# An adaLN block: chunk 2's statistics into a product buffer, chunk 5's norm and DMA transpose placed earlier, chunk 7's turns on TensorE

## The chip, the cores and the metric

The kernel runs on one core of one Trainium2 chip. The metric is the device time in microseconds (us) of one execution. The core has five engines that run their own queues of instructions in order: PE (TensorE, the matrix unit; its weight loads are listed apart as PEld), DVE (VectorE), ACT (ScalarE), POOL (GpSimd) and SP (SyncE, here a queue that issues DMAs). POOL issues DMAs too. SBUF is the working memory with 128 partitions; PSUM has eight banks, in which PE leaves its results.

## The reference

```
mod = silu(c) @ w_mod                      # six rows of 576: sa, ca, ga, sb, cb, gb
h = layernorm(x) * (1 + ca) + sa           # x: 2048 x 576
qkv = h @ wqkv                             # 32 heads of 18
attn = softmax over 8 keys at positions s, s-2, ..., s-14 of q.k / sqrt(18)
x = x + ga * ((attn . v) @ wo)
h = layernorm(x) * (1 + cb) + sb
x = x + gb * (((h @ w_gate) * (h @ w_up)) @ w_down)     # 576 -> 4608 -> 576
```

## The kernel before

**Tiling.** The 2048 rows are eight chunks of 256 rows (`CH`), each of two tiles of 128 (`ST`). The attention goes chunk by chunk; the second half (the GLU) goes by five groups of row tiles, `GROUPS` (line 45): 2, 4, 4, 3 and 3 tiles. For each group `gate_up` (line 879) runs 36 steps f over the 4608 columns, and then `down_pairs` (line 936; `down_last` for the last group) multiplies by `w_down`, in steps n: 32 or 48 steps and a last block of four f. Nearly all matmuls are pairs: one on rows 0 to 63 of the array and one on rows 64 to 127, side by side.

**The order of the work is written out by hand.** The program is compiled with a manual schedule: each engine keeps the order in which the code emits its instructions, and the waits between engines follow from the tiles. The attention of later chunks is woven into the GLU of earlier groups. `gbg[gi]` (lines 1397 to 1401) is a list of pieces with costs; `spread` (line 869) places them over the 36 steps of `gate_up` by running cost. `units` (lines 1508 to 1510) puts q, k and v projections of later chunks behind given steps f. `dbg[gi]` (lines 1496 to 1507) puts pieces behind given steps n of `down_pairs`. So a number such as 27 in `(27, a_flip(4))` is a place in the emitted order, not a time: an engine with nothing else in its queue may come to the piece earlier.

**Pieces.** `a_` pieces belong to the first layernorm and the projections of a chunk, `b_` pieces to the attention and the second layernorm, `o_` to the attention's output. A normalised chunk (tile `ln_xn`) has to be transposed before it can be multiplied. There are two ways. A *turn* is done on PE: `turn_unit` (line 606) makes 20 transposes of 64x64 output blocks for two row tiles, 12 in its first part and 8 in its second, into two PSUM banks (`tr_pA`, `tr_pB`), and its evictions by ACT and DVE also apply the modulation (`o_parts`, `a_parts`, `b_parts`). A *flip* is a DMA transpose on SP's queue, one for each row tile (`flips`, line 690, with `o_flip`, `a_flip`, `b_flip`), and the modulation comes later, in place (`a_mod`, `b_mod`). The attention's logits are transposed the same two ways: `b_lq` (line 480) leaves them in `lgs` and, for chunks over 2, issues a flip to `lgt`; for chunks 1 and 2 `b_lt` (line 501) makes eight transposes on PE and two ACT copies.

**Buffers.** `lnp` (line 78) has two buffers for `ln_xn`; chunks over 2 also put their eighth product there (line 467 on, `b_p`). `prodp` has six product buffers, `hTp` one `hT`, `h2p` one `h2T`, and `psp` the eight PSUM banks. When a tile is made, the compiler gives it a buffer that an earlier tile has given back, and the first instruction that writes the new tile waits for the last readers of the old one.

**Around the change.** Near the end of group 0's `down_pairs`, `norm_x1_2` (line 1479) computes chunk 2's second layernorm: row tile 0's mean and squares on ACT (`act_norm`, line 306, which uses its own output tile `xn` as the place for the values that nobody reads), row tile 1's on DVE, and then the norm of both on DVE. Two evictions of chunk 3's values follow on ACT (`v1_3`), then chunk 1's turns (`b_parts(1)`, places 27 and 28), the flips of chunk 4's norm (`a_flip(4)`, place 27) and chunk 2's own turns (`t2_2`, from place 30). In group 1's `gate_up`, `B_both` (line 853) goes through chunks 3 and 4: products, logits, softmax (`B_sm`), weighted values; chunk 5's first layernorm (`a_ln(5)`, `a_norm(5)`) comes behind chunk 3's weighted values and its flips in chunk 4's softmax, and its projections at f = 29 to 33. In group 3's `down_pairs` come chunk 7's output flips, its projection `w7` by `wo`, its layernorm and flips, and the flip of chunk 6's second row tile. With three row tiles this stage holds six PSUM banks (`acc` and `accr`) and has two left.

Of the kernel before, what the change touches and what calls it, by code (L numbers as in the profile page):

```python
# [18 lines left out]
P = 128  # L19
D = 576  # L20
# [21 lines left out]
MODK = (0, 4, 1, 2, 3)  # L42
QKK = (0, 1, 4, 2, 3)
PAIRED = (3, 4, 5, 6, 7)
GROUPS = [(0, 2), (2, 6), (6, 10), (10, 13), (13, 16)]


@with_exitstack
def kernel(
# [253 lines left out]
        nc.scalar.activation(rstd, rstd, ACTF.Ln, bias=eps[:], scale=1.0 / D)  # L303
        nc.scalar.activation(rstd, rstd, ACTF.Exp, scale=-0.5)

    def act_norm(src):
        xn = lnp.tile([P, ST, DP], BF, name="ln_xn")
        mv = small.tile([P, ST, 2], F32, name="ln_mva")

        def mean(j):  # L310
            nc.scalar.activation(xn[:, j, 0:D], src(j), ACTF.Identity, scale=-1.0 / D, accum_out=mv[:, j, 0:1])

        def square(j):
            nc.scalar.activation(xn[:, j, 0:D], src(j), ACTF.Square, bias=mv[:, j, 0:1], accum_out=mv[:, j, 1:2])

        def rsq(r=slice(0, ST)):
            nc.scalar.activation(mv[:, r, 1], mv[:, r, 1], ACTF.Ln, bias=eps[:], scale=1.0 / D)
            nc.scalar.activation(mv[:, r, 1], mv[:, r, 1], ACTF.Exp, scale=-0.5)

        def norm(j):  # L320
            for d0, s0, n in ((0, 0, D), (D, D - 64, 64)):
                nc.vector.tensor_scalar(xn[:, j, d0:d0 + n], src(j)[:, s0:s0 + n], mv[:, j, 0:1], mv[:, j, 1:2], ALU.add, ALU.mult)
        return xn, mean, square, rsq, norm
# [156 lines left out]
    def b_lq(i, wq):  # L480
        b = bb[i]
        if wq == 0:
            b["lg"] = ps([P, 2, CH], F32, "lg")
        for m in range(KT):
            for wl in range(4):
                nc.tensor.matmul(b["lg"][H * wl:H * (wl + 1), wq, :], lhsT=ind[:, m, :], rhs=b["prod"][4 * wq + wl][:, m, :],  # L486
                                 start=(m == 0), stop=(m == KT - 1), skip_group_check=True)
        for wl in range(4):
            b["prod"].pop(4 * wq + wl)
        if wq == 1:  # L490
            lgs = lgp.tile([P, 2, CH], BF, name="lgs")
            nc.scalar.copy(lgs[:], b.pop("lg")[:])
            b["lgt"] = lgp.tile([P, 2, ST, 4, H], BF, name="lgt")
            if i > 2:
                nc.sync.dma_start_transpose(out=b["lgt"][:].rearrange("p a j w h -> p (a j) (w h)"), in_=lgs[:].rearrange("p a t -> p (a t)"))
            else:
                b["lgs"] = lgs
# [1 line left out]
    LO, HI = slice(0, 64), slice(64, P)  # L499

    def b_lt(i):
        if i > 2:
            return
        b = bb[i]
        lgs = b.pop("lgs")
        pts = [ps([P, 2 * ST, 64], BF, "lt") for _ in range(2)]
        for a in range(2):
            for j in range(ST):
                for pt, r in zip(pts, (LO, HI)):
                    nc.tensor.transpose(pt[:, ST * a + j, :], lgs[r, a, js(j)], ident[r, r])  # L510
        for k, pt in enumerate(pts):
            nc.scalar.copy(b["lgt"][:].rearrange("p a j w h -> p (a j) (w h)")[:, :, 64 * k:64 * (k + 1)], pt[:])
# [191 lines left out]
    def a_mod(i):  # L704
        return lambda: in_place(aa[i]["hT"], 0, KT)
# [127 lines left out]
    def B_pr(i, w0, w1):  # L833
        return [(0.83, lambda w=w: b_p(i, w)) for w in range(w0, w1)]
# [14 lines left out]
    def b_lqs(i):  # L849
        b_lq(i, 0)  # L850
        b_lq(i, 1)

    def B_both(first, a, b, av_a, av_b, *turned):
        return (B_pr(a, 0, 3) + [(0.0, p) for p in first] + B_pr(a, 3, 8) + B_wait(1.5) + [(0.0, lambda: b_lqs(a))] + B_wait(1.5) + B_pr(b, 0, 8) + B_wait(1.5)
                + B_sm(a, lambda: b_lqs(b)) + av_a + B_sm(b, *turned) + av_b)

    def B_one(a, ld, av_a):
        return (B_pr(a, 0, 4) + ld[:1] + B_pr(a, 4, 8) + ld[1:] + B_wait(1.5) + [(0.0, lambda: b_lqs(a))] + B_wait(4.0) + B_sm(a) + av_a)
# [530 lines left out]
    def values(i):  # L1389
        return [(0.0, lambda: [b_ld(i, j) for j in range(ST)])]  # L1390

    av1 = B_av(1)
    for k, p in ((13, lambda: n3["square"](1)), (11, lambda: mean3(1)), (8, lambda: n3["square"](0)), (5, lambda: mean3(0))):
        av1.insert(k, (0.0, p))
    av4 = B_av(4)
    av4.insert(6, (0.5, a_mod(5)))
    gbg = {0: B_two(1, 2, av1 + [res(2), (0.0, load_wm5), (0.0, lambda: load_wd(0))], []),
           1: values(3) + B_both([a_mod(4)], 3, 4, B_av(3) + [res(3), res(4), (2.4, lambda: a_ln(5)), (1.2, lambda: (a_norm(5), load_x(7)))], av4, o_flip(3), a_flip(5)),
           2: values(5) + B_both((), 5, 6, B_av(5) + [res(5), res(6)], B_av(6), nop, o_flip(5)),
           3: B_one(7, [(0.0, lambda: b_ld(7, 0)), (0.0, lambda: behind(b_ld(7, 1), wgu_in[3 * NBLK + 4]))], B_av(7)) + [res(7)],  # L1400
           4: [(1.0, nop), (1.0, early_wd)]}
    av2 = [p for _, p in B_av(2)]
# [74 lines left out]
        n4["rsq"]()  # L1477

    def norm_x1_2():
        begin(n2, lambda j: x1[2][j][:])  # L1480
        xn = bb[2]["xn"] = n2["xn"]
        stats, mv = small.tile([P, ST, 2, 6], F32, name="ln_statsb"), small.tile([P, ST, 2], F32, name="ln_mvb")
        stat_act(n2, (0,))
        n2["rsq"](slice(0, 1))
        for hf in range(2):
            nc.vector.bn_stats(stats[:, 1, hf, :], x1[2][1][:, hf * 288:(hf + 1) * 288])
# [3 lines left out]
        n2["norm"](0)  # L1490
        for d0, s0, n in ((0, 0, D), (D, D - 64, 64)):
            nc.vector.tensor_scalar(xn[:, 1, d0:d0 + n], x1[2][1][:, s0:s0 + n], mv[:, 1, 0:1], mv[:, 0, 1:2], ALU.subtract, ALU.mult)
# [56 lines left out]
```

## Time and profile before

| | us |
|---|---|
| three runs | 552.82, 561.39, 565.06 |
| their median | 561.39 |
| the profiled execution | 557.14 |
| its span, first to last instruction | 555.4 |
| `gate_up`, group 0 (from 47.1) | 39.6 |
| `down_pairs`, group 0 (from 86.7) | 40.7 |
| `gate_up`, group 1 (from 127.4) | 89.4 |
| `down_pairs`, group 1 (from 216.8) | 39.7 |
| `gate_up`, group 2 (from 256.5) | 79.2 |
| `down_pairs`, group 2 (from 335.7) | 39.7 |
| `gate_up`, group 3 (from 375.4) | 61.0 |
| `down_pairs`, group 3 (from 436.4) | 35.7 |
| `gate_up`, group 4 (from 472.1) | 52.7 |
| `down_last` (from 524.8) | 30.6 |

How the lines are read: in a timeline a line gives the start in us, the length in us, the engine, the line of the code, the operation, output <- inputs, and how many equal instructions are merged (x4, say); the bracket at its end is the idle time of the engine ahead of it and what ended that. In a view by stretches of time each engine has its busy time and (x) its instructions, then the granted share of PE's clock (PEclk; 1.00 is full), the busy share of the DMA engines and what they moved. In the list of waits each line is an engine's instruction and what it waited for, with the total in us, the number of times and the longest.

### The profile page before, as it was taken

What the parts mean: (1) busy time and instruction counts of PE and PEld (TensorE: products, weight loads), DVE (VectorE), ACT (ScalarE), POOL (GpSimd) and SP (SyncE); (2) the same over time, 40 slices, a digit from 0 to 9 for tenths busy, and PEclk for the clock granted to TensorE, in tenths of its full rate; (3) what the DMA queues carried; (4) which work ended last, traced back from release to release, by engine and by line L of the source; (5) the groups of instructions that cost most, each with busy time, mean ns of one, the idle gap of its engine ahead of it and who ended that gap; (6) DMA issues with size and microseconds to landing.
All of it is one profiled execution on the core that took longest, in us unless ns stands there. A gap on an engine that the chain in (4) does not pass through costs nothing.

```text
span 555.4 us, 16882 instructions
## 1 busy us (share of the span) xinstructions
PE 533.4 (96%) x7253; PEld 341.7 (62%) x7259; DVE 317.5 (57%) x775; ACT 256.1 (46%) x617; POOL 71.1 (13%) x117
## 2 busy tenths in 40 slices
PE   7999999959999979999999999999999979999997
PEld 5788886635544456656644445557655768777664
DVE  7887899747369855656366795725429322422202
ACT  2766787644655654111655552205556301455500
POOL 4301223021000000122000101111100112200010
PEclk9999999979999999999999999999999989999999
DMA  8999998969265945966635896763896858965021
GB/s 275 271 294 313 355 295 285 336 130 334 80 172 180 292 119 170 181 173 215 225 109 139 269 261 151 181 165 106 271 245 218 206 134 229 318 212 182 2 87 33
DMA packets 92310, 114.05 MB, mean 205 GB/s; under 512 B 25770, under 2 KB 79994, under 8 KB 92234
## 3 DMA queue, kind: packets, MB, share of 16 engines
q1 hardware_dynamic: 80976, 67.00, 44.3%
q0 software_dynamic: 11168, 45.81, 26.6%
q8 instruction: 57, 0.93, 0.7%
q14 instruction: 19, 0.16, 0.1%
q10 hardware_dynamic: 90, 0.15, 0.1%
HBM read 103.22 MB, written 4.48 MB: 194 GB/s over the span
## 4 chain that ended last, share of the span: by engine, by line
PE 83%; DMA 6%; issue 4%; DVE 3%; ACT 2%; SPq 1%; POOL 1%; ACTq 0%; POOLq 0%
PE pg L563 26%; PE pu L563 21%; PE acc L563 15%; PE pp L563 8%; PE acc L1078 3%; PE accr L563 2%; DMA wgu<-in_B_w_up_dram 2%; PE lg L486 2%; DMA hT<-ln_xn 1%; DMA wqk<-in_A_wqkv_dram 1%; SPq L692 1%; DMA wd<-in_B_w_down_dram 1%; DVE prod L476 1%; PE pq L415 1%; PE po L791 1%
## 5 line engine op out<-in xcount | busy, mean ns | idle before, releaser
L563 PE MATMUL pg<-h2T,wgu 64*128 64x512 bf16 (+2 forms) x1440 | 280.3, 334 | 0.0
L563 PE MATMUL pu<-h2T,wgu 64*128 64x512 bf16 (+2 forms) x1440 | 276.2, 334 | 0.2 <-DMA wgu<-in_B_w_up_dram 0.2
L563 PEld LDWEIGHTS <-wgu 64*128 64x128 bf16 x2880 | 148.4, 94 | 99.1 <-issue 0.7
L906 ACT CAST u_sb<-pu 128x512 bf16<-128x512 f32 (+2 forms) x180 | 90.1, 501 | 141.2 <-PE pg L563 133.0
L912 DVE TENSOR_TENSOR hh<-g_sb,u_sb 128x512 bf16<-128x512 bf16 (+2 forms) x180 | 66.3, 370 | 106.5 <-ACT g_sb L907 104.6
L563 PE MATMUL acc<-wd,hh 64*128 64x512 bf16 x888 | 117.2, 380 | 0.7 <-DMA wd<-in_B_w_down_dram 0.6
L563 PEld LDWEIGHTS <-hh 64*128 64x128 bf16 x1872 | 75.7, 96 | 41.8 <-issue 2.0
L907 ACT CAST g_sb<-pg 128x512 bf16<-128x512 f32 (+2 forms) x180 | 91.5, 509 | 0.0
L563 PE MATMUL accr<-wd,hh 64*128 64x64 bf16 x888 | 85.5, 191 | 0.0
L563 PE MATMUL pu<-h2T,wgr 64*128 64x512 bf16 (+2 forms) x180 | 60.2, 335 | 0.0
L563 PE MATMUL pg<-h2T,wgr 64*128 64x512 bf16 (+2 forms) x180 | 60.2, 334 | 0.0
L173 POOL DMA_DIRECT2D wd<-in_B_w_down_dram x38 | 28.8, 758 | 172.1 <-PE accr L563 94.3
L476 DVE TENSOR_TENSOR prod<-qT,kT 128x1280 bf16<-128x1280 bf16 x54 | 42.9, 820 | 7.8 <-ACT kT L393 7.8
L548 DVE TENSOR_TENSOR vsh<-vsh,attn 128x1152 bf16<-128x1152 bf16 x56 | 40.2, 751 | 0.0
L563 PEld LDWEIGHTS <-wgr 64*128 64x128 bf16 x360 | 19.8, 94 | 13.8 <-issue 2.0
L661 DVE TENSOR_TENSOR x<-pp,ga_bc 128x288 bf16<-128x288 f32 x28 | 12.0, 452 | 25.0 <-PE pp L563 25.0
L563 PE MATMUL pp<-hT,wqk 64*128 64x256 bf16 x360 | 22.5, 269 | 3.2 <-DMA hT<-ln_xn 3.0
L563 PE MATMUL pp<-wo,oT 64*128 64x288 bf16 x252 | 21.5, 291 | 4.2 <-DMA oT<-o_sb 4.2
L563 PEld LDWEIGHTS <-wqk 64*128 64x128 bf16 x360 | 18.0, 94 | 7.2 <-DMA hT<-ln_xn 3.4
L281 ACT ACTIVATE ln_rstdb<-ln_mvb,eps 128x2 f32<-128x2 f32 (+1 forms) x6 | 1.8, 296 | 41.3 <-DVE ln_mvb L278 41.3
L560 POOL COPY o_sb<-o_sb 128x64 bf16<-128x64 bf16 x10 | 3.0, 296 | 138.7 <-DVE o_sb L559 138.7
L329 ACT ACTIVATE h2T<-h2T,modc 128x256 bf16<-128x256 bf16 (+1 forms) x12 | 6.1, 557 | 31.1 <-DMA h2T<-ln_xn 31.1
(269 smaller groups left out, 563.9 us busy)
## 6 DMA issues: line engine op xcount, KB each, us to landing
wgu<-in_B_w_gate_dram SPq DMA_DIRECT2D x45, 512.0 KB, 4.3
wgu<-in_B_w_up_dram SPq DMA_DIRECT2D x45, 512.0 KB, 6.5
wd<-in_B_w_down_dram POOLq DMA_DIRECT2D x38, 576.0 KB, 4.7
vsh<-vd POOLq DMA_DIRECT2D x14, 1152.0 KB, 8.7
x_r<-in_A_x_dram SPq DMA_DIRECT2D x8, 288.0 KB, 6.9
vsh<-in_B_w_down_dram POOLq DMA_DIRECT2D x4, 576.0 KB, 7.1
out_dram<-x SPq DMA_DIRECT2D x15, 144.0 KB, 6.8
x_t<-in_A_x_dram SPq DMA_DIRECT2D x7, 288.0 KB, 8.3
```

The source lines that it names most:

```text
L173: return nc.gpsimd.dma_start(wb[:], B_w_down[r0:r0 + FB * P, :].rearrange("(k p) n -> p k n", p=P))
L329: nc.scalar.activation(dst, s, ACTF.Identity, bias=modc[:, vi_shift, m:m + 1], scale=modc[:, vi_scale, m:m + 1])
L415: nc.tensor.matmul(pq[:, gi, :], lhsT=qk_w(kt, m), rhs=hT[:, kt, :], start=(kt == 0), stop=(kt == KT - 1))
L476: nc.vector.tensor_tensor(prod[:], aa[i]["qT"][:], aa[i]["kT"][:, :, off:off + CH], ALU.mult)
L486: nc.tensor.matmul(b["lg"][H * wl:H * (wl + 1), wq, :], lhsT=ind[:, m, :], rhs=b["prod"][4 * wq + wl][:, m, :], start=(m == 0), stop=(m == ...
L548: nc.vector.tensor_tensor(v, v, at, ALU.mult)
L563: return nc.tensor.matmul(dst, lhsT=lhs, rhs=rhs, start=first, stop=last, skip_group_check=True)
L661: nc.vector.tensor_tensor(x1[i][j][:, cs], t[:, 0, :], ga_bc[:, cs], ALU.mult)
L906: nc.scalar.copy(u[:, 0:N], pu[:, 0:N])
L907: nc.scalar.copy(g[:, 0:N], pg[:, 0:N])
L912: nc.vector.tensor_tensor(hh[:, f, 0:N], g[:, 0:N], u[:, 0:N], ALU.mult)
L1078: nc.tensor.matmul(a[:], lhsT=hh[:, f, js(j)], rhs=wb[:, f % FB, cs], start=(f == 0), stop=(f == FT - 1))
```

## The change

Four things are edited.

1. `act_norm` takes another tile for the values that nobody reads. `norm_x1_2` gives it a product buffer (`prodp`) and makes its `ln_xn` tile after that; the first to write that tile is now DVE's norm. `a_flip(4)` goes from place 27 to place 29.
2. In group 1's `gate_up`, `a_ln(5)` (bn_stats on DVE) takes the place of a wait ahead of chunk 3's softmax, `a_norm(5)`, the load of chunk 7's x and `a_flip(5)` go ahead of the second half of that softmax, and `a_mod(5)` goes behind chunk 3's weighted values. In group 2, `o_flip(5)` is emitted a little earlier in chunk 6's softmax.
3. `TURNED_BY_DMA` leaves chunk 7 out, so chunk 7's logits are transposed on PE.
4. In group 3's `down_pairs` all flips are replaced by turns: those of chunk 7's output, of chunk 6's second row tile and of chunk 7's second layernorm; the places are new.

```
+TURNED_BY_DMA = (3, 4, 5, 6)
...
-    def act_norm(src):
-        xn = lnp.tile([P, ST, DP], BF, name="ln_xn")
+    act_mv = []
+
+    def act_norm(src, junk=None):
+        xn = lnp.tile([P, ST, DP], BF, name="ln_xn") if junk is None else None
+        junk = xn if junk is None else junk
         mv = small.tile([P, ST, 2], F32, name="ln_mva")
+        act_mv.append(mv)
 
         def mean(j):
-            nc.scalar.activation(xn[:, j, 0:D], src(j), ACTF.Identity, scale=-1.0 / D, accum_out=mv[:, j, 0:1])
+            nc.scalar.activation(junk[:, j, 0:D], src(j), ACTF.Identity, scale=-1.0 / D, accum_out=mv[:, j, 0:1])
...
-            if i > 2:
+            if i in TURNED_BY_DMA:
                 nc.sync.dma_start_transpose(out=b["lgt"][:].rearrange("p a j w h -> p (a j) (w h)"), in_=lgs[:].rearrange("p a t -> p (a t)"))
...
     def b_lt(i):
-        if i > 2:
+        if i in TURNED_BY_DMA:
             return
...
-    def B_both(first, a, b, av_a, av_b, *turned):
-        return (B_pr(a, 0, 3) + [(0.0, p) for p in first] + B_pr(a, 3, 8) + B_wait(1.5) + [(0.0, lambda: b_lqs(a))] + B_wait(1.5) + B_pr(b, 0, 8) + B_wait(1.5)
-                + B_sm(a, lambda: b_lqs(b)) + av_a + B_sm(b, *turned) + av_b)
+    def B_both(first, a, b, av_a, av_b, turned, stat=None, norm=None):
+        sm_a = B_sm(a, lambda: b_lqs(b))
+        if norm:
+            sm_a[3] = (1.2, norm)
+        return (B_pr(a, 0, 3) + [(0.0, p) for p in first] + B_pr(a, 3, 8) + B_wait(1.5) + [(0.0, lambda: b_lqs(a))] + B_wait(1.5) + B_pr(b, 0, 8)
+                + ([(2.0, stat)] if stat else B_wait(1.5)) + sm_a + av_a + B_sm(b, turned) + av_b)
...
-    av4 = B_av(4)
-    av4.insert(6, (0.5, a_mod(5)))
...
-           1: values(3) + B_both([a_mod(4)], 3, 4, B_av(3) + [res(3), res(4), (2.4, lambda: a_ln(5)), (1.2, lambda: (a_norm(5), load_x(7)))], av4, o_flip(3), a_flip(5)),
-           2: values(5) + B_both((), 5, 6, B_av(5) + [res(5), res(6)], B_av(6), nop, o_flip(5)),
+           1: values(3) + B_both([a_mod(4)], 3, 4, B_av(3) + [res(3), res(4), (0.0, a_mod(5))], B_av(4), o_flip(3),
+                                   lambda: a_ln(5), lambda: (a_norm(5), load_x(7), a_flip(5)())),
+           2: values(5) + B_both((), 5, 6, B_av(5) + [res(5), res(6)], B_av(6), o_flip(5)),
...
     def norm_x1_2():
-        begin(n2, lambda j: x1[2][j][:])
-        xn = bb[2]["xn"] = n2["xn"]
+        src = lambda j: x1[2][j]
+        junk = prodp.tile([P, ST, DP], BF, name="prod")
+        _, mean, square, rsq, _ = act_norm(lambda j: src(j)[:], junk)
+        xn = bb[2]["xn"] = lnp.tile([P, ST, DP], BF, name="ln_xn")
...
-                 (24, norm_x1_2), (25, v1_3), (27, b_parts(1)), (27, a_flip(4)), (FT - FB - 2, t2_2)),
+                 (24, norm_x1_2), (25, v1_3), (27, b_parts(1)), (29, a_flip(4)), (FT - FB - 2, t2_2)),
...
-           3: at((0, o_flip(7)), (0, b_flip(6, (1,))), (10, b_mod(6, (1,))), *apart(14, w7[0]), *apart(19, w7[1]), (22, lambda: b_ln(7)),
-                 (29, lambda: b_norm(7)), (32, b_flip(7)), (45, b_mod(7)))}
+           3: at(*apart(3, b_parts(6, (1,))), *apart(9, o_parts(7)), *apart(16, w7[0]), *apart(23, w7[1]), (27, lambda: b_ln(7)),
+                 (33, lambda: b_norm(7)), *apart(41, b_parts(7)))}
```

(`apart(n, parts)` puts a unit's first part at place n and its second at n + 2.)

More of the change, by code (lines that the diff above doesn't have):

```diff
@@ L304, in mean_var_on_act @@
         nc.scalar.activation(rstd, rstd, ACTF.Exp, scale=-0.5)
-    def act_norm(src):
-        xn = lnp.tile([P, ST, DP], BF, name="ln_xn")
+    act_mv = []
+    def act_norm(src, junk=None):
+        xn = lnp.tile([P, ST, DP], BF, name="ln_xn") if junk is None else None
+        junk = xn if junk is None else junk
         mv = small.tile([P, ST, 2], F32, name="ln_mva")
+        act_mv.append(mv)
         def mean(j):
-            nc.scalar.activation(xn[:, j, 0:D], src(j), ACTF.Identity, scale=-1.0 / D, accum_out=mv[:, j, 0:1])
+            nc.scalar.activation(junk[:, j, 0:D], src(j), ACTF.Identity, scale=-1.0 / D, accum_out=mv[:, j, 0:1])
         def square(j):
-            nc.scalar.activation(xn[:, j, 0:D], src(j), ACTF.Square, bias=mv[:, j, 0:1], accum_out=mv[:, j, 1:2])
+            nc.scalar.activation(junk[:, j, 0:D], src(j), ACTF.Square, bias=mv[:, j, 0:1], accum_out=mv[:, j, 1:2])
         def rsq(r=slice(0, ST)):
@@ L1479, in norm_x1_2 @@
     def norm_x1_2():
-        begin(n2, lambda j: x1[2][j][:])
-        xn = bb[2]["xn"] = n2["xn"]
+        src = lambda j: x1[2][j]
+        junk = prodp.tile([P, ST, DP], BF, name="prod")
+        _, mean, square, rsq, _ = act_norm(lambda j: src(j)[:], junk)
+        xn = bb[2]["xn"] = lnp.tile([P, ST, DP], BF, name="ln_xn")
+        mva = act_mv[-1]
         stats, mv = small.tile([P, ST, 2, 6], F32, name="ln_statsb"), small.tile([P, ST, 2], F32, name="ln_mvb")
-        stat_act(n2, (0,))
-        n2["rsq"](slice(0, 1))
+        mean(0)
+        square(0)
+        rsq(slice(0, 1))
         for hf in range(2):
-            nc.vector.bn_stats(stats[:, 1, hf, :], x1[2][1][:, hf * 288:(hf + 1) * 288])
+            nc.vector.bn_stats(stats[:, 1, hf, :], src(1)[:, hf * 288:(hf + 1) * 288])
         nc.vector.bn_aggr(mv[:, 1, :], stats[:, 1].rearrange("p a b -> p (a b)"))
@@ L1489, in norm_x1_2 @@
         nc.scalar.activation(mv[:, 0, 1:2], mv[:, 0, 0:1], ACTF.Exp, scale=-0.5)
-        n2["norm"](0)
-        for d0, s0, n in ((0, 0, D), (D, D - 64, 64)):
-            nc.vector.tensor_scalar(xn[:, 1, d0:d0 + n], x1[2][1][:, s0:s0 + n], mv[:, 1, 0:1], mv[:, 0, 1:2], ALU.subtract, ALU.mult)
+        for j, m, r, op in ((0, mva[:, 0, 0:1], mva[:, 0, 1:2], ALU.add), (1, mv[:, 1, 0:1], mv[:, 0, 1:2], ALU.subtract)):
+            for d0, s0, n in ((0, 0, D), (D, D - 64, 64)):
+                nc.vector.tensor_scalar(xn[:, j, d0:d0 + n], src(j)[:, s0:s0 + n], m, r, op, ALU.mult)
     q3, k3, qk4_3, v0_3, v1_3 = qkv_units(3, [(0, 0, 5)])[0]
```

## The prediction

> **What bounds the kernel now.** I read the page's busy times first, then PE's waits, then windows around the long waits.
>
> ```profile
> span 555.4 us, 16882 instructions
> ...
> PE 533.4 (96%) x7253; PEld 341.7 (62%) x7259; DVE 317.5 (57%) x775; ACT 256.1 (46%) x617; POOL 71.1 (13%) x117
> ```
>
> PE is busy 96% of the span. A faster ACT or DVE is worth nothing here; only two things are: the 22 us in which PE stands still, and the time in which it runs at a lower clock.
>
> ```profile
> PE tr_pA L610 <- ACT v_sb L746: 6.3, 1, 6.3
> PE pp L563 <- DMA oT<-o_sb: 4.2, 1, 4.2
> PE pp L563 <- DMA hT<-ln_xn: 3.0, 1, 3.0
> ...
> PE acc L563 <- DMA wd<-in_B_w_down_dram: 0.6, 1, 0.6
> ...
> PE pp L563 <- ACT hT L329: 0.2, 1, 0.2
> ```
>
> Three waits stand out, and the change has one part for each. What follows a wait counts too:
>
> ```profile
> 115.30:121.80 6.50, 0.20 (x5) 0.10 (x1) 0.72 (x3) 2.87 (x10) 0.00 (x0) 0.66 0.46 36
> 121.80:127.40 5.60, 5.51 (x60) 2.78 (x61) 2.68 (x10) 2.89 (x7) 5.10 (x7) 0.50 0.65 193
> 194.30:197.30 3.00, 0.04 (x4) 0.05 (x4) 3.00 (x6) 1.07 (x2) 0.00 (x0) 1.00 0.92 187
> 197.30:202.00 4.70, 4.70 (x70) 3.78 (x72) 0.75 (x2) 1.67 (x4) 0.00 (x0) 1.00 0.63 215
> 444.10:448.30 4.20, 0.01 (x1) 0.00 (x0) 0.00 (x0) 0.00 (x0) 0.00 (x0) 1.00 1.11 195
> 448.30:453.00 4.70, 4.69 (x49) 3.77 (x51) 1.49 (x5) 0.88 (x2) 0.00 (x0) 0.64 0.29 94
> ```
>
> The columns are the length, busy PE, PEld, DVE, ACT, POOL, then PE's clock. After 6.3 us of idleness PE runs at 0.50 for 5.6 us: 2.8 us lost. After 4.2 us it runs at 0.64 for 4.7 us: 4.7 x 0.36 = 1.7 lost. After 3.0 us the clock stays at 1.00. So the waits cost 9.1, 5.9 and 3.0 us.
>
> **Part 1, chunk 2's statistics (the 6.3 us wait).**
>
> ```profile
> 113.05 2.62 SPq L692 DMA_TRANSPOSE hT<-ln_xn  x2
> ```
> ```profile
> 112.36 0.65 PE L563 MATMUL pp<-wv,hT 64*128 64x288 bf16 x8
> ...
> 114.00 0.19 PE L610 MATMUL tr_pB<-ident,ln_xn 64*128 64x64 bf16 x1
> ...
> 121.80 0.21 PE L610 MATMUL tr_pA<-ident,ln_xn 64*128 64x64 bf16 x1 [6.30 <-ACT v_sb L746]
> ```
> ```profile
> 118.81 0.68 ACT L311 ACTIVATE ln_xn<-x 128x576 bf16<-128x576 bf16 x1 [10.68 <-DMA hT<-ln_xn]
> ...
> 121.37 0.68 ACT L746 CAST v_sb<-pp 128x288 bf16<-128x288 f32 x2
> ```
> ```profile
> 111.47 0.46 DVE L663 TENSOR_TENSOR x<-x,x_r 128x576 bf16<-128x576 bf16 x1
> ...
> 121.08 0.64 DVE L322 TENSOR_SCALAR ln_xn<-x,ln_mva 128x576 bf16<-128x576 bf16 x2 [7.20 <-ACT ln_mva L318]
> ```
>
> ```profile
> 122.04 1.10 POOL L749 DMA_DIRECT2D vd<-v_sb  x2 [19.67 <-ACT v_sb L746]
> 123.14 2.25 POOL L173 DMA_DIRECT2D wd<-in_B_w_down_dram  x3
> ```
>
> Chunk 2's input is there at 111.9, but ACT starts its mean at 118.8, because the new `ln_xn` takes the buffer of chunk 4's norm, which flips are still reading. The value evictions are queued behind it on ACT, and PE's next turn waits for their banks. With a product buffer for the unread values, ACT starts at 112.0; the evictions come 2.6 us later, as in the rows (118.81 to 121.37), at 114.6. ACT's part is gone. The wait does not vanish: DVE's norm still writes an `lnp` buffer, and now DVE waits for it, with chunk 1's three DVE evictions queued behind. Which buffer? SP issued the flips at 113.05, just after the last value matmul that reads `hT` (112.36 + 0.65), and not at their place in the code; nothing else stands on SP between places 27 and 29. So I expect them at 113.05 again, ahead of chunk 1's second turns at 114.00, and chunk 4's buffer is again the one given. Then DVE starts when the flips land, by the ACT row at 118.7; the turn follows DVE by 0.7 (121.08 to 121.80), at 119.4 instead of 121.8. But POOL's value writes and three weight loads, so far queued behind those evictions, now run beside the flips; I add 0.5, between nothing and the slow flips of part 3. PE gains 1.9. The idle time from 115.5 is then 4.4 us, between the two long ones above, so the clock loses about 2.2 instead of 2.8. Sum: **2.4** (3.5 if the flips are undisturbed and the clock does as after the 4.2 us wait; -2.6 if they land as late as part 3's).
>
> **Part 2, chunk 5's norm and flips (the 3.0 us wait).**
>
> ```profile
> 164.23 0.64 ACT L528 ACTIVATE dd<-dd 128x512 f32<-128x512 f32 x1
> ...
> 185.60 0.31 ACT L281 ACTIVATE ln_rstda<-ln_mva,eps 128x2 f32<-128x2 f32 x1
> ```
> ```profile
> 191.94 3.77 SPq L692 DMA_TRANSPOSE hT<-ln_xn  x2
> ```
>
> The norm moves from ACT's 185.6 to just behind chunk 3's exponential at 164, its costs in the list shrinking from 52.9 to 50.1; by cost it stands at step 15.4 of 36, and the projections at 29. The flips, issued at 191.9 behind chunk 3's output flips, go some 20 us earlier, so even the slow case of 9.2 us (part 3) is hidden. `a_mod(5)` stands at step 24.9, ahead of the first projection; before, by cost, at 31. DVE's work is the same in sum. On SP, one load, two flips and the weight loads behind them wait for DVE's norm, a few us; the weight blocks are loaded two blocks ahead. Gain **3.2**: 3.0 and 0.2 of other waits of these units. If the cover failed it would be nothing. Group 2's `o_flip(5)`: nothing, no PE wait stands there.
>
> **Part 3, chunk 7 (the 4.2 us wait).**
>
> ```profile
> 437.75 3.36 SPq L692 DMA_TRANSPOSE oT<-o_sb  x2
> 441.16 22.23 SPq L692 DMA_TRANSPOSE h2T<-ln_xn  x3
> ```
> ```profile
> DMA to landing us min/median/max: 9.2/9.2/9.2
> ```
> ```profile
> 113.34 0.19 PE L610 MATMUL tr_pA<-ident,ln_xn 64*128 64x64 bf16 x1
> ...
> 113.51 0.38 PE L563 MATMUL acc<-wd,hh 64*128 64x512 bf16 x2
> ```
> ```profile
> 60.96 0.28 PE L510 MATMUL lt<-ident,lgs 64*128 64x64 bf16 x8
> 61.17 0.73 PE L486 MATMUL lg<-prod,ind 128*32 128x256 bf16 x20
> ```
> ```profile
> 443.79 0.28 PE L563 MATMUL pp<-wo,oT 64*128 64x288 bf16 x1
> ```
> ```profile
> 106.10 0.58 ACT L646 COPY oT<-tr_pA 128x512 bf16<-128x512 bf16 x1 [1.13 <-PE tr_pA L610]
> ...
> 107.22 0.30 ACT L649 COPY oT<-tr_pB 128x128 bf16<-128x128 bf16 x1
> ```
> ```profile
> 455.83 0.46 DVE L661 TENSOR_TENSOR x<-pp,ga_bc 128x288 bf16<-128x288 f32 x1 [2.73 <-PE pp L563]
> ...
> 460.13 1.18 DVE L286 TENSOR_SCALAR ln_xn<-x,ln_mvb,ln_rstdb 128x576 bf16<-128x576 bf16 x4 [0.60 <-ACT ln_rstdb L282]
> ```
>
> The output flips take 9.2 us to land; PE needs them 6 us after their issue. Removed: six flips on SP (one for the logits). Added on PE: 20 + 10 + 20 turns and eight for the logits. Twelve turns took PE 0.17 us (113.34 to 113.51), so 50 cost 0.7; the logits' eight 0.21: together 1.0. ACT's and DVE's evictions take the place of in-place modulations, on engines that stand idle here. The stage has two free banks, so each unit waits for the one before to be evicted. A step lasts (443.8 - 436.4) / 15 = 0.49 us. The longest eviction (ACT, 106.10 to 107.52) is 1.4, against five steps, 2.4 us, from place 11 to 16; from `w7`'s last part to chunk 7's norm took 455.8 to 461.3, 5.5 us, and there are 15 steps, 7.3 us. All fits. The 0.6 us wait for `wd`, late in this stage, stands behind the last of the flips (issued until 463.4) and should go with them. Gain: 4.2 + 1.7 + 0.6 - 1.0 = **5.5** (3.5 if two handovers of banks and the `wd` load each wait 0.7; 6.0 at best).
>
> Against this speaks a rule of the Trainium skill (TensorE: Matmul & The Clock Gate, Part 4: PE-mode transpose): about 275 ns for one 128x128 transpose in a kernel, 390 ns alone. By it the 58 turns would cost 16 to 23 us, an estimate. The row above has twelve smaller ones in 0.17 us.
>
> **The sum.** 2.4 + 3.2 + 5.5 = 11.1; the span falls to 544.3. The profiled execution took 557.14, 1.7 more than its span: **546.0 us**, 2.0% less. That execution is 0.8% under the median of the three runs, 561.39; the same share off that would be 550.
>
> **Rivals.**
> - *Chunk 1's buffer is given.* The code now has chunk 1's second turns (place 28) ahead of the flips (29). If the compiler goes by that, DVE is free at 114.3, the turn goes at 115.5 with no wait, and the clock never falls: 9.1 instead of 2.4, so 539. For it: the code order; against it: SP's issue at 113.05. Chance 24%.
> - *Late flips.* Beside the weight loads, chunk 4's flips land after 9.2 us as those of part 3 did (the second of the two goes half way through the issue row of 2.62 us, at 114.4; 114.4 + 9.2 = 123.6): PE loses 2.6 instead of gaining 2.4, so 551. Chance 12%.
> - *Turns one at a time.* If PE cannot overlap the turns of chunk 7 as it did those of chunk 1, each costs at least its record, 0.19 us: 58 make 11.0 and the time is 556; at 0.24, its record behind the long wait (below), 13.9 and 559, the gain gone. It decides at 12.1 / 58 = 0.21 us for one turn. Chance 2%. By the 275 to 390 ns that the Trainium skill has for one transpose (TensorE: Matmul & The Clock Gate, Part 4) it would be 561 to 568, an estimate; the trace is against it.
>
> ```profile
> 122.15 0.24 PE L610 MATMUL tr_pA<-ident,ln_xn 64*128 64x64 bf16 x1
> ```
>
> - *Two banks are too few.* In group 3's `down_pairs` PE stands still at the handovers so long, each time like the 4.2 us above, that its clock stays at 0.50: the stage of 30 us takes 60, and the time is 576, slower by 3.4%. It decides when the stage loses the whole 11.1, at a clock of 30 / 41 = 0.73. Against it: the longest eviction is 1.4 us, and 3.0 us of idleness left the clock at 1.00. Chance 4%.
> - The rest is the forecast: 58%.
>
> **How the numbers follow.** A measurement of this kernel tells about 2% from no change; its three runs lie 2.2% apart. The forecast, 2.0% less, lies on that bound, so its 58% is split: 34 for faster by over 2% (the better bounds of parts 1 and 3 lie there, and they are the cases in which nothing new goes wrong) and 24 for within. The first rival adds its 24 to faster: 58%. The late flips add 12 to within, the serial turns 2: 38%. The two banks are the 4% for slower. The forecast's own range is 543 to 551, from the bounds of parts 1 and 3. The range of 8 in 10 goes from 538, under the first rival, to 554, over the second and over the median's 550.
>
> **What would show it.** Right: no wait of PE for `oT`, none for `hT` near step 29, PE at 1.00 through group 3's `down_pairs`, that stage near 30 us; PE still idle some 4 us ahead of chunk 2's turns, with DVE's norm (not ACT) waiting for the flips. Wrong: DVE's norm starts at 114 (first rival); turns spaced by 0.2 us; PE waiting for evictions in group 3's `down_pairs`, or weight loads late in group 1's `gate_up`.

## The result, and the profile after

The median of six runs of the changed kernel is 547.07 us (545.34 to 548.96); six runs of the kernel before beside them have a median of 558.62 us (551.79 to 565.28). The ratio is 0.988, with a 95% interval of 0.983 to 0.993; it leaves out executions of a kernel that took over 1.5% more than its fastest, which is why it is nearer to 1 than the ratio of the two medians, 0.979. The forecast was 546.0. The profiled execution took 545.34 us, its span 543.6.

The page's line of busy times, and the list of PE's waits, of the changed kernel:

```profile
PE 532.2 (98%) x7317; PEld 319.6 (59%) x7317; DVE 317.2 (58%) x775; ACT 258.9 (48%) x625; POOL 72.3 (13%) x117
```
```profile
PE tr_pA L615 <- DVE ln_xn L1503: 4.6, 1, 4.6
PE idle L209 <- DVE hT L204: 1.3, 1, 1.3
PE pq L1213 <- DMA wqk<-in_A_wqkv_dram: 0.9, 2, 0.5
PE pm L1171 <- DMA wmA<-in_w_mod_dram: 0.2, 1, 0.2
```

The waits for `oT`, `hT` and `wd` are gone. The wait ahead of chunk 2's turns is still there, shorter (4.6 for 6.3) and with another releaser: DVE's norm, not ACT's eviction. The other three stand in the start-up. Now the same stretches as before, by windows (length, busy PE, PEld, DVE, ACT, POOL, then PE's clock):

```profile
115.90:120.60 4.70, 0.07 (x4) 0.00 (x0) 0.47 (x2) 1.11 (x3) 2.45 (x4) 0.77 0.94 179
120.60:125.90 5.30, 5.19 (x62) 2.62 (x64) 2.94 (x11) 1.37 (x3) 2.51 (x3) 0.56 0.76 236
125.90:211.70 85.80, 85.80 (x983) 44.64 (x981) 58.90 (x126) 51.08 (x106) 5.13 (x10) 1.00 0.73 188
431.00:460.40 29.40, 29.40 (x522) 16.15 (x520) 8.81 (x26) 5.55 (x16) 6.32 (x9) 1.00 0.64 188
```

The first two rows are what is left of group 0's wait and the low clock behind it. In group 1's `gate_up` (third row) and group 3's `down_pairs` (fourth) PE is busy all the time, at full clock. The timelines of the end of group 0's `down_pairs` show the new wait, engine by engine:

```profile
112.49 0.68 ACT L316 ACTIVATE prod<-x 128x576 bf16<-128x576 bf16 x1 [3.89 <-DVE x L668]
...
115.06 0.68 ACT L751 CAST v_sb<-pp 128x288 bf16<-128x288 f32 x2
```
```profile
113.52 2.62 SPq L697 DMA_TRANSPOSE hT<-ln_xn  x2
```
```profile
120.13 0.64 DVE L1503 TENSOR_SCALAR ln_xn<-x,ln_mva 128x576 bf16<-128x576 bf16 x2 [5.78 <-DMA hT<-ln_xn]
```
```profile
120.61 0.23 PE L615 MATMUL tr_pA<-ident,ln_xn 64*128 64x64 bf16 x1 [4.64 <-DVE ln_xn L1503]
```

ACT starts its mean as soon as the input is there and has the values evicted at 115.7; DVE then stands idle 5.8 us until the flips of chunk 4 have read their buffer. The three stages named became 2.0, 3.6 and 6.2 us shorter; the others kept their length within 0.3 us, and the start-up ahead of them took 0.5 us longer.

### The profile page after: what moved, and what is told of

Same layout as the page of the kernel before. It is cut to its first block, busy times and chain, and to the rows that moved or that the text cites. A ratio compares the mean times of both kernels' runs of the same rounds, so it can differ in the third digit from the quotient of the medians.

```text
span 543.6 us, 17000 instructions
## 1 busy us (share of the span) xinstructions
PE 532.2 (98%) x7317; PEld 319.6 (59%) x7317; DVE 317.2 (58%) x775; ACT 258.9 (48%) x625; POOL 72.3 (13%) x117
## 4 chain that ended last, share of the span: by engine, by line
PE 92%; DVE 3%; DMA 2%; ACT 1%; SPq 1%; issue 1%; DVEq 0%; ACTq 0%
PE pg L568 29%; PE pu L568 23%; PE acc L568 18%; PE pp L568 9%; PE acc L1086 4%; PE accr L568 2%; PE lg L491 2%; DMA wqk<-in_A_wqkv_dram 1%; DVE prod L481 1%; DMA hT<-ln_xn 1%; PE pq L420 1%; PE pq L1213 1%; PE po L796 1%; PE pv L445 1%; PE accr L1090 1%
## 5 line engine op out<-in xcount | busy, mean ns | idle before, releaser
L568 PEld LDWEIGHTS <-wgu 64*128 64x128 bf16 x2880 | 140.6, 94 | 104.9 <-issue 0.2
L568 PE MATMUL acc<-wd,hh 64*128 64x512 bf16 x888 | 115.8, 378 | 0.1
L568 PEld LDWEIGHTS <-hh 64*128 64x128 bf16 x1872 | 62.4, 95 | 51.9 <-issue 1.8
L568 PE MATMUL accr<-wd,hh 64*128 64x64 bf16 x888 | 77.1, 189 | 0.0
L568 PEld LDWEIGHTS <-wgr 64*128 64x128 bf16 x360 | 17.8, 94 | 14.4 <-issue 1.7
L560 DVE TENSOR_TENSOR vsh<-vsh 128x1152 bf16<-128x1152 bf16 x28 | 20.4, 751 | 0.0
L568 PE MATMUL pp<-wo,oT 64*128 64x288 bf16 x252 | 19.9, 283 | 0.0
```

The lines of the kernel that those rows point to most:

```text
L560: nc.vector.tensor_tensor(vsh[:, d], vsh[:, d], vsh[:, 4 + 2 * s:6 + 2 * s], ALU.add)
L568: return nc.tensor.matmul(dst, lhsT=lhs, rhs=rhs, start=first, stop=last, skip_group_check=True)
```

## The experiments

The stages that matter, in all profiles, in us. A stage lasts from its first matmul to that of the next stage; "idle" is PE's idle time ahead of chunk 2's turns. The labels are those of the experiments below.

| kernel | idle | `down_pairs` 0 | `gate_up` 1 | `down_pairs` 3 |
|---|---|---|---|---|
| before | 6.30 | 40.70 | 89.43 | 35.62 |
| before, second profile (e9) | 6.51 | 40.10 | 88.36 | 41.89 |
| before + output's turns (e5) | 6.09 | 40.30 | 88.89 | 35.09 |
| the same, modulation later (e8) | 6.14 | 39.59 | 88.91 | 30.14 |
| before + part 1 (e1) | 4.06 | 37.80 | 88.54 | 39.22 |
| the same, second profile (e10) | 4.64 | 39.26 | 89.21 | 31.29 |
| after, without part 2 (e2) | 4.72 | 38.89 | 88.46 | 29.39 |
| after | 4.64 | 38.68 | 85.83 | 29.39 |
| after, second profile (e11) | 5.03 | 39.65 | 85.90 | 29.39 |
| after, flips at place 27 (e4) | 4.04 | 37.85 | 86.42 | 29.39 |
| after, more turns (e6) | 4.56 | 38.97 | 86.17 | 31.14 |
| after, flips behind turns (e7) | none | 31.28 | 85.83 | 29.39 |
| after, norm in a product buffer (e3) | none | 30.99 | 85.83 | 29.39 |

**e3: chunk 2's norm in a product buffer too.** The edit of the changed kernel:

```
-        xn = bb[2]["xn"] = lnp.tile([P, ST, DP], BF, name="ln_xn")
+        xn = bb[2]["xn"] = prodp.tile([P, ST, DP], BF, name="prod")
```

> The changed kernel, with chunk 2's norm too in a tile of the product pool instead of an lnp buffer, so that DVE has nothing to wait for. Theory (the 4.64 us in which PE still stands idle ahead of chunk 2's turns, and the 5.3 us at a clock of 0.56 behind it, come from DVE's wait for chunk 4's flips): DVE's norm starts near 114.5, the first turn follows near 115.5-116.0 with at most 0.5 us of idle time, the clock stays at 1.00, and the stage is shorter by 4.64 + 5.3 x 0.44 = 7.0 us: span near 536.7, time near 538.4, 1.3% under the changed kernel. Rival one (PE waits there for the value evictions on ACT, or for POOL, and the wait for the flips only covers it): the idle time stays above 2 us and the gain is under 4 us. Rival two (the tile of the product pool is late in turn, since its users are the pooling products): DVE or POOL waits for it and the time is within 1 us of the changed kernel's.

Measured: 538.75 us median of four runs (537.63 to 539.08), 0.962 of the kernel before (interval 0.956 to 0.969); span 537.3. PE's waits, DVE's row of the norm, and the whole of group 0's `down_pairs`:

```profile
PE idle L209 <- DVE hT L204: 1.3, 1, 1.3
PE pm L1171 <- DMA wmA<-in_w_mod_dram: 1.3, 3, 0.6
PE pg L568 <- issue: 1.0, 1, 1.0
PE pq L1213 <- DMA wqk<-in_A_wqkv_dram: 0.6, 1, 0.6
```
```profile
115.54 0.64 DVE L1503 TENSOR_SCALAR prod<-x,ln_mva 128x576 bf16<-128x576 bf16 x2 [0.41 <-ACT ln_mva L323]
```
```profile
88.50:119.50 31.00, 30.89 (x590) 20.05 (x588) 26.40 (x67) 22.27 (x65) 8.46 (x12) 1.00 1.02 291
```

The wait is gone, the clock stays at 1.00, and the stage is 38.68 - 30.99 = 7.7 us shorter, a little over the 7.0 expected. The two rivals fall: neither ACT's evictions nor the product pool hold the turns up. This is the fastest version of the study: the waits left in PE's list are in the first 12 us, and one of 1.0 us near 82.

**e7: the flips behind chunk 1's turns.** The norm stays in `lnp`; chunk 4's flips wait for the last of chunk 1's turns, so that chunk 1's buffer comes free first (`behind` adds the dependency):

```
+            r = nc.sync.dma_start_transpose(out=aa[4]["hT"][:, :, js(j)], in_=aa[4]["xn"][:, j, :])
+            if j == 0:
+                behind(r, last_turn[0])
```

> The changed kernel, with chunk 4's flips made to wait for chunk 1's last turn, which takes a fraction of a microsecond from their issue. Theory (which of two lnp buffers comes free first decides what chunk 2's norm gets: chunk 4's, read by flips until 120, or chunk 1's, read by turns until 114): the norm now gets chunk 1's, starts near 114.5, and the idle time of 4.64 us and the low clock behind it go: 7.0 us less, time near 538.4; chunk 4's flips are issued some 0.5 to 2 us later, and nothing waits for them. Rival (the buffers go round in a fixed order, or by the order of the code): the norm still waits for the flips, which are now later, and the idle time grows by 0.5 to 2 us: 546 to 549.

Measured: 539.42 us median of four runs (538.30 to 540.43), 0.963 of before (0.956 to 0.971); span 538.7. SP's and DVE's timelines:

```profile
115.82 3.39 SPq L1513 DMA_TRANSPOSE hT<-ln_xn  x2
```
```profile
115.90 0.64 DVE L1505 TENSOR_SCALAR ln_xn<-x,ln_mva 128x576 bf16<-128x576 bf16 x2 [0.55 <-PE tr_pA L617]
```

The releaser in DVE's bracket is now a turn of PE. The flips go later and nothing waits for them. So it is the order in which two buffers of `lnp` come free that decides the wait: this is the case of the first rival of the prediction, made on purpose.

**e4: chunk 4's flips back at place 27.**

```
-(27, b_parts(1)), (29, a_flip(4))
+(27, b_parts(1)), (27, a_flip(4))
```

> The changed kernel, with chunk 4's flips back at place 27, ahead of chunk 1's second turns in the code, as before the change. Theory (SP issues them just behind the last value matmul that reads hT, wherever they stand between places 27 and 29): nothing moves; idle time ahead of chunk 2's turns 4.6 us, first turn at 120.6, span within 0.5 us of 543.6. Rival (the place in the code sets when they are issued): they go up to 1 us earlier, land earlier, and the idle time is 0.5 to 1.0 us shorter.

Measured: one run, 547.21 us, span 545.5; idle 4.04. SP's and DVE's timelines:

```profile
114.37 2.62 SPq L697 DMA_TRANSPOSE hT<-ln_xn  x2
```
```profile
120.38 0.64 DVE L1503 TENSOR_SCALAR ln_xn<-x,ln_mva 128x576 bf16<-128x576 bf16 x2 [5.18 <-DMA hT<-ln_xn]
```

The stage begins at 88.05 here and at 87.19 in the changed kernel, so the flips are issued 26.3 us into it in both (114.37 - 88.05; 113.52 - 87.19). Whether they stand at place 27 or 29 does not matter. The idle time is 0.6 us shorter, which is what the rival expected, but not because of an earlier issue: the second flip landed 4.6 us after its issue here and 5.2 in the changed kernel, and in e1, with the flips at place 29, 4.6 as well. The span misses what was expected, 543.6 within 0.5: the start-up takes 0.9 us more than in the changed kernel, group 1's `gate_up` 0.6 and the last stage 1.1.

**e1: the first part alone**, on the kernel before: `act_norm` and `norm_x1_2` as in the change, and

```
-            nc.scalar.activation(xn[:, j, 0:D], src(j), ACTF.Identity, scale=-1.0 / D, accum_out=mv[:, j, 0:1])
+            nc.scalar.activation(junk[:, j, 0:D], src(j), ACTF.Identity, scale=-1.0 / D, accum_out=mv[:, j, 0:1])
...
-(27, b_parts(1)), (27, a_flip(4))
+(27, b_parts(1)), (29, a_flip(4))
```

> The kernel before, with only the first part of the change (chunk 2's statistics write into a product buffer; chunk 4's flips at place 29). Theory (the parts act each in its own stage and add up): group 0's down_pairs shorter by 2.0 us as in the changed kernel, the waits for hT (3.0 us, group 1's gate_up) and oT (4.2 us, group 3's down_pairs) still there and unchanged: span 553.4. Rival (the parts depend on one another through the order of the buffers, so that part of the 2.0 us came from another part): under 1 us less or over 3 us less in that stage, or one of the other two waits changed by more than 0.5 us.

Measured: one run, 557.02 us, span 555.3. PE's waits:

```profile
PE pp L567 <- DMA oT<-o_sb: 7.3, 2, 5.6
PE tr_pA L614 <- DVE ln_xn L1500: 4.1, 1, 4.1
PE pp L567 <- DMA hT<-ln_xn: 2.1, 1, 2.1
```

Group 0's `down_pairs` fell by 2.9 us and yet the span did not: the wait for `oT` had grown from 4.2 to 7.3 us. By its letter that is the rival's case. Three kernels without any edit tell more, each in a second profile: the kernel before (e9), that with the first part (e10) and the changed one (e11).

> The kernel before, unchanged, profiled a second time, to see what its three waits do from one execution to the next. In the kernel with the first part alone, group 0's down_pairs was 2.9 us shorter than before, but the wait for oT in group 3's down_pairs had grown from 4.2 to 5.6 + 1.7 us and the one for hT had shrunk from 3.0 to 2.2, so that the span did not fall. Theory (these waits end with the landing of flips, which differs from execution to execution): in this second profile of the same program the wait for oT or its low clock differs from the first by 0.5 us or more, the wait for hT by 0.3 us or more, and the span by 1 us or more. Rival (the first part of the change lengthens the wait for oT, through the order of the buffers): this profile repeats 6.3, 3.0 and 4.2 us within 0.2.

> The kernel with the first part of the change alone, profiled a second time. Theory (the long wait for oT was that execution's): the wait for oT lies elsewhere in 3 to 8 us, by over 0.5 us from the 5.6 + 1.7 of the first look; group 0's down_pairs lies again 2 to 3 us under the 40.3-40.7 of the kernels without the first part. Rival (the first part itself lengthens that wait): 5.6 + 1.7 us again, within 0.2.

> The changed kernel, unchanged, profiled a second time. Theory (of the waits that end with a flip only the one ahead of chunk 2's turns is left, so that alone moves from execution to execution): that idle time lies in 4.0 to 5.2 us, group 0's down_pairs in 37.8 to 39.3, every stage from group 1's down_pairs on within 0.3 us of the first profile: span 542.5 to 545.5. Rival (the scatter of the kernel before comes from the chip as a whole, such as the clock): the later stages move by over 0.5 us too.

Measured: the kernel before 561.48 us (span 559.7), with the first part 552.06 (550.4), the changed one 545.90 (544.2). In e9 all that the theory expected came: the waits for `oT` and `hT` and the span differ from the first profile by 4.8, 1.0 and 4.3 us. PE's longest waits in the second profile of the kernel before, and then in that of the kernel with part 1:

```profile
PE pp L563 <- DMA oT<-o_sb: 9.0, 2, 5.3
PE tr_pA L610 <- ACT v_sb L746: 6.5, 1, 6.5
PE pp L563 <- DMA hT<-ln_xn: 2.0, 1, 2.0
```
```profile
PE tr_pA L614 <- DVE ln_xn L1500: 4.6, 1, 4.6
PE pp L567 <- DMA hT<-ln_xn: 2.8, 1, 2.8
...
PE pp L567 <- DVE x L665: 0.7, 1, 0.7
```

The same program waits 4.2 us for `oT` in one execution and 9.0 in another; with part 1 it waits 7.3 or not at all. The list of DMA issues (last number: us from issue to landing) has for chunk 7's output flips 9.2 in the first profile of before, and then, in the second, in e1 and in e10:

```profile
oT<-o_sb SPq DMA_TRANSPOSE x2, 14.2
```
```profile
oT<-o_sb SPq DMA_TRANSPOSE x2, 12.5
```
```profile
oT<-o_sb SPq DMA_TRANSPOSE x2, 4.3
```

So the dependence on part 1 falls, and the first theory's idea of an unchanged wait with it. Between the two profiles of the kernel before, the stages with the three waits differ by 6.3, 1.1 and 0.6 us and group 3's `gate_up` by 0.4; each other stage repeats within 0.05 us. e10 missed what was expected of it twice: it has no wait for `oT` at all, and its group 0 stage, 39.26, is only 1.0 to 1.4 us under the 40.3 to 40.7 it was measured against. In e11 the idle time (5.03) fits, the stage (39.65) is 0.35 longer than allowed for, and everything from group 1 on repeats: 85.90 for 85.83 and 29.39 for 29.39. The scatter is not the chip's as a whole. What makes the same flips land after 4.3 us in one execution and 14.2 in another is not settled. It is not the flips alone that are late: the load of a `w_up` block, issued on SP just ahead of them, landed after 5.1, 8.0, 7.4 and 5.1 us where they took 9.2, 14.2, 12.5 and 4.3.

**e2: the changed kernel without part 2** (`B_both` and group 2's list too are as before):

```
-           1: values(3) + B_both([a_mod(4)], 3, 4, B_av(3) + [res(3), res(4), (0.0, a_mod(5))], B_av(4), o_flip(3),
-                                   lambda: a_ln(5), lambda: (a_norm(5), load_x(7), a_flip(5)())),
+           1: values(3) + B_both([a_mod(4)], 3, 4, B_av(3) + [res(3), res(4), (2.4, lambda: a_ln(5)), (1.2, lambda: (a_norm(5), load_x(7)))], av4, o_flip(3), a_flip(5)),
```

> The changed kernel without its second part: chunk 5's statistics, norm, turned blocks and flips are put back to where group 1's list had them before. Theory (the 3.0 us for hT are the whole of what the second part removed, as a wait and not as a change of clock): a wait for hT of 2 to 3.8 us (3.0 before, 2.15 in the kernel with the first part alone) comes back in group 1's gate_up with the clock at 1.00 behind it, that stage grows from 85.8 to 88.0-89.4 us, all other stages stay within 0.5 us: span 546 to 547.2. Rival (the earlier norm also took engine time or loads out of the way, or costs some elsewhere): the stage grows by more than the wait that comes back, by 1 us or over, or group 1's or 2's down_pairs change.

Measured: one run, 549.10 us, span 547.4. PE's waits and the whole of group 1's `gate_up`:

```profile
PE pp L568 <- DMA hT<-ln_xn: 2.1, 1, 2.1
...
PE pp L568 <- ACT hT L334: 0.2, 1, 0.2
```
```profile
126.30:214.80 88.50, 86.20 (x984) 46.29 (x982) 59.82 (x126) 51.23 (x106) 5.00 (x10) 1.00 0.61 182
```

The stage grows by 88.46 - 85.83 = 2.6 us, of which 2.3 are the two waits that come back; the clock is 1.00. Part 2 is this wait and hardly more. The span is 0.2 us over the range expected, since the last stage took 0.7 more than in the changed kernel, 0.5 of it a wait for `wd`.

**e5: only the output's turns, on the kernel before.** The other four flips of group 3 stay, and chunk 6's modulation stays at place 10; chunk 7's further steps move to about the places of the changed kernel:

```
-           3: at((0, o_flip(7)), (0, b_flip(6, (1,))), (10, b_mod(6, (1,))), *apart(14, w7[0]), *apart(19, w7[1]), (22, lambda: b_ln(7)),
-                 (29, lambda: b_norm(7)), (32, b_flip(7)), (45, b_mod(7)))}
+           3: at((0, b_flip(6, (1,))), *apart(9, o_parts(7)), (10, b_mod(6, (1,))), *apart(16, w7[0]), *apart(23, w7[1]), (27, lambda: b_ln(7)),
+                 (33, lambda: b_norm(7)), (34, b_flip(7)), (46, b_mod(7)))}
```

> The kernel before, with only chunk 7's attention output turned on TensorE (20 turns in group 3's down_pairs in place of its two flips, and chunk 7's further steps at the places of the changed kernel); the flips of chunk 6's and chunk 7's second norms and of chunk 7's logits stay. Theory (the wait for oT and the low clock behind it are what the flips cost): both are gone, group 3's down_pairs falls from 35.6 us to 29.4-30.2, and what is left over the changed kernel's 29.4 is the wait for the weight blocks of 0.6 to 0.8 us, since four flips are still ahead of them on SP. Rival (the other flips cost as much, by landing late or by holding up the weight loads behind them on SP): the stage stays over 31 us, with PE waiting for h2T or wd.

Measured: one run, 555.73 us, span 554.0; the stage takes 35.09 us, a miss for the theory. ACT's timeline, and the windows of the wait and behind it:

```profile
445.68 0.88 ACT L329 ACTIVATE h2T<-h2T,modc 128x128 bf16<-128x128 bf16 x2 [8.62 <-DMA h2T<-ln_xn]
446.47 0.56 ACT L646 COPY oT<-tr_pA 128x512 bf16<-128x512 bf16 x1
...
447.57 0.28 ACT L649 COPY oT<-tr_pB 128x128 bf16<-128x128 bf16 x1
```
```profile
444.67:447.90 3.23, 0.00 (x0) 0.00 (x0) 0.76 (x3) 2.17 (x6) 0.00 (x0) 1.00 0.84 285
447.90:453.00 5.10, 5.09 (x56) 2.73 (x58) 0.82 (x2) 0.00 (x0) 0.75 (x1) 0.67 0.29 70
```

The turns were done at 442; their evictions stood on ACT behind a modulation that waits for another flip until 445.7, and PE waited for the evictions. The rival is right that the other flips matter. e8 tells by which way:

```
-*apart(9, o_parts(7)), (10, b_mod(6, (1,))), *apart(16, w7[0]), *apart(23, w7[1]), (27, lambda: b_ln(7)),
+*apart(9, o_parts(7)), *apart(16, w7[0]), *apart(23, w7[1]), (24, b_mod(6, (1,))), (27, lambda: b_ln(7)),
```

> The kernel before with only chunk 7's output turned on TensorE, as in the run before, but with the in-place modulation of chunk 6's second blocks at place 24 in place of 10, behind the evictions of the turns. In the run before the output's evictions stood on ACT and DVE behind that modulation, which waits for flips until 445.7, and PE waited 3.2 us for them with a clock of 0.67 behind. Theory (the flips of h2T cost by what is queued behind the instruction that waits for them, and not by their own lateness): PE's wait for oT and the low clock behind it are gone, group 3's down_pairs falls from 35.1 to 29.4-30.2 us, the rest over the changed kernel's 29.4 being the wait for wd of 0.6 us; span 548.2 to 549.2. Rival (the flips hold up the stage in another way too, by their transfers or by the weight loads behind them on SP): a wait of PE of over 1 us stays, for wd, h2T or an eviction, and the stage stays over 31 us.

Measured: one run, 549.72 us, span 548.0. ACT's timeline and the whole stage:

```profile
441.22 0.59 ACT L646 COPY oT<-tr_pA 128x512 bf16<-128x512 bf16 x1 [5.20 <-PE tr_pA L610]
...
442.49 0.90 ACT L329 ACTIVATE h2T<-h2T,modc 128x128 bf16<-128x128 bf16 x2
```
```profile
434.80:465.00 30.20, 29.52 (x493) 17.32 (x489) 8.57 (x27) 4.98 (x14) 6.30 (x9) 1.00 0.82 214
```

With the evictions ahead of the modulation the stage takes 30.14 us, 0.75 over the changed kernel's, and 0.5 of that is the wait for `wd` (the span is 0.2 us under the range expected). A caveat: here the flips had landed by the time ACT came to the modulation, so this run had luck as well as the better order; but in neither order was it `h2T` itself that PE waited for.

**e6: forty turns done four times over.**

```
-            for c, j in enumerate(cols):
+            for c, j in list(enumerate(cols)) * times:
```

> The changed kernel, with the turns of chunk 7's output and of its second norm done four times over, the same block into the same place of the bank: 40 turns become 160, all else as it is. This is extra work that measures the price of one turn. Theory (PE overlaps them as it did chunk 1's twelve in 0.17 us, 0.014 us each): group 3's down_pairs and the start of group 4's gate_up grow by 120 x 0.014 = 1.7 us, span 545.3. Rival one (a turn costs its record, 0.19 us): 120 x 0.19 = 23 us, span 566. Rival two (the Trainium skill, TensorE: Matmul & The Clock Gate, Part 4: PE-mode transpose, 275 ns in a kernel and 390 ns alone): 33 to 47 us, an estimate, span 577 to 590. [...]

Measured: one run, 548.45 us, span 546.7. Group 3's `down_pairs`:

```profile
432.30:463.40 31.10, 31.10 (x638) 17.88 (x636) 8.75 (x26) 5.55 (x16) 6.32 (x9) 1.00 0.61 178
```

The stage grows by 31.14 - 29.39 = 1.75 us for 120 turns: 0.0146 us each, as the theory had it. The span is 1.4 us over its 545.3, and that lies ahead of this stage, in the start-up and the next three stages (0.3 us in each). A record's 0.19 us is the length of one turn, not what it takes from PE: turns overlap, as chunk 1's twelve in 0.17 us did. The 275 to 390 ns that the Trainium skill has for one 128x128 transpose (TensorE: Matmul & The Clock Gate, Part 4: PE-mode transpose) are no price for a turn in this kernel. The clock stayed at 1.00 with 170 turns in this stage.

## Why the prediction came out right, point by point

**Part 1.** The mechanism is as forecast in each step: ACT's part went, DVE waits for chunk 4's flips, SP issues them just behind the last value matmul from either place (e4: 114.37, behind 114.34), chunk 4's buffer is given (e7 shows what the other gives), and the idle time is near the 4.4 us forecast: 4.04 to 5.03 in seven profiles, mean 4.53. The step that failed is "the clock loses about 2.2 instead of 2.8", which lets the loss shrink with the idle time. The undisturbed stage takes 31.0 us (e3). Taking that and the idle time off the table's `down_pairs` 0 leaves a mean of 2.9 us in the four profiles without part 1 and 3.2 in the seven with it: an idle time of 4.0 us loses as much as one of 6.5. Windows cut where the clock changes show what happens, here for the kernel before, the changed one and e4 (PE's clock is the third number from the end; it is 1.00 on either side of each):

```profile
117.32:127.56 10.24, 5.67 (x62) 3.03 (x64) 3.41 (x12) 5.75 (x16) 5.10 (x7) 0.50 0.39 115
```
```profile
118.45:125.28 6.83, 4.57 (x56) 2.37 (x58) 3.38 (x12) 1.37 (x3) 2.41 (x3) 0.50 0.76 240
```
```profile
121.74:125.15 3.41, 3.41 (x44) 1.72 (x42) 1.71 (x7) 1.37 (x3) 2.10 (x3) 0.50 0.61 174
```

The low clock comes in stretches of 3.41 us: three, two and one. What PE loses is half of what falls behind its restart (at 121.80, 120.61 and 120.87): 2.9, 2.3 and 1.7 us. In e9, after the longest idle time, it is a stretch of 6.83 us of which 3.84 fall behind the restart, so 1.9. By this measure too the mean is 2.5 both without part 1 and with it. So the 2.2 was a fair size, and what was wrong is the 2.8, taken from one profile as what a longer wait costs. Part 1 was worth 40.17 - 38.73 = 1.4 us by the table's means, not 2.4 (the prediction's own terms, 1.9 and 0.6, make 2.5), and what it left standing was worth 7.7.

**Part 2.** Forecast 3.2. By the means of the table (seven profiles without it, 88.83, and six with it, 86.00) it is 2.8. It was sized by one execution, in which the wait was 3.0; it was 2.0 to 2.8 in the six others. The flips go 23 us earlier (168.8 for 191.9), and no new wait of PE appears, as forecast.

**Part 3.** Forecast 5.5. Against the first profile the stage gave 35.62 - 29.39 = 6.2. The turns cost what the working said: 50 x 0.0146 = 0.7, and the logits' eight 0.12, by group 3's `gate_up` of 60.60 us in e9 and 60.72 after, for the forecast 0.21. (The forecast's 0.7 and 0.21 make 0.9; the prediction took 1.0.) What the first profile gave beyond the sum is not the clock: without waits and turns the stage takes 29.39 - 0.73 = 28.66, so before it lost 35.62 - 4.20 - 0.59 - 28.66 = 2.2 us besides its waits, of which the low clock (0.50 from 448.42 to 451.83) is 1.7, as priced; the other 0.5 stays open. The two free banks were enough, even at four times the turns. What the prediction did not see is that its 4.2 us was one draw: the four profiles with these flips have 31.29 to 41.89 us for the stage, mean 37.0, so that the part gives 1.9 to 12.5 us, 7.6 on average. With four profiles that spread so far, the 7.6 is a rough size.

**The sum.** 1.4 + 2.8 + 7.6 = 11.8 by means, for 11.1 forecast; the medians of the runs differ by 558.62 - 547.07 = 11.55. The mechanisms were right, but that the total fits is luck: part 1 was taken 1.0 too high, part 2 0.4 too high and part 3 2.1 too low. By the ratio of 0.988 the change is worth only some 6.7 us (1.2% of 558.62), which is within 2%; the prediction had put 38% on that and 58% on faster by more. It set its sum against the profiled execution's 557.14, which is close to the later median of before, 558.62; against the 561.39 of three runs it would have been 550.

**Rivals.** *Chunk 1's buffer is given*: it was not; its price was right (539 forecast; e7 539.4). *Late flips*: in the seven profiles that have the wait for them DVE starts 6.0 to 7.0 us after the issue of the first of chunk 4's flips, and neither flip took 9.2 us to land. *Turns one at a time*: 0.0146 us each (e6). *Two banks are too few*: PE has no wait in group 3's `down_pairs`, with the turns as they are or four times over.

**The scatter.** Runs of the kernel before lie within 552 to 565 us, those of the changed one within 545 to 549, and the two versions without the group 0 wait within 1.5 and 2.1 us. The flips still land late in the changed kernel. The view of the tile `oT` of the changed kernel:

```profile
L697 SPq DMA_TRANSPOSE oT<-o_sb x8: 1201/1763/5331, 185.1 to 339.2; - x8
...
DMA to landing us min/median/max: 3.2/8.7/18.7
```

But the eight that are left belong to chunks 3 to 6, and PE waits for none of them. The change took out the two that had no slack.

## What to carry to other kernels

Size a wait that ends with a DMA by several profiles of the same program before you price its removal: here one profile said 4.2 us and the next 9.0, while the later stages of the changed kernel repeated within 0.1 us. When a wait only gets shorter, ask whether it also gets short enough for the clock to stay up (here 3.0 us was, 4.0 was not); going from 6.3 to 4.6 us was worth 1.4 us, and taking the rest away 7.7. An instruction that waits for a late transfer costs whatever is queued behind it on its engine, so put the evictions that PE needs ahead of it.

## What the runs showed of the hardware that was not expected

- What the stage loses behind an idle time did not follow how long that was: 2.7 us after 4.06 (e1), 3.6 after 5.03 (e11), 2.6 after 6.51 (e9), each over the 31.0 us of the undisturbed stage. In group 0's `down_pairs` the low clock lasted 10.24 us (before), 6.83 (e9, after) or 3.41 (e1, e4). It began 1.8 us after PE fell idle in the first profile of before (117.32 against 115.50), and in e4 only 0.9 us after PE had gone back to work.
- Idle times of PE of 2.1 to 3.0 us left the clock at 1.00 (e2, before); one of 3.23 us was followed by 0.76 us at 1.00 and then 3.41 us at 0.50 (e5). The Trainium skill (TensorE: Matmul & The Clock Gate, Part 1: The HAM clock gate) says that the clock is halved after one idle window or more, of about 3.4 us, and restored after a busy one, and that the windows run freely. The stretches of 3.41 us agree with that; e5's idle time is a little under the window.
- The low clock does not account for all that the stage lost: in the changed kernel for 2.3 us of 38.68 - 4.64 - 30.99 = 3.05. What the rest is was not shown; the stage without any wait took 30.99 us in e3 and 31.28 in e7, so that part of it can be scatter.
- Flips of the same size landed after 2.6 us (the fastest, of `hT`) to 18.7 us (of `oT`), in one execution of the changed kernel.
- A turn of 64x64 takes 0.0146 us of PE's time beside a record of 0.19 us (e6).
